# Order of attention blocks, the bank of the last half block and the width of the setup's constant matmuls in a fused attention and feed-forward kernel

## Chip, core and metric

The kernel runs on one core of a Trainium2 chip. The metric is the device time of one execution in microseconds (us), lower is better. Engines are named as in the profile: PE is the matrix engine (TensorE), PEld its weight loads, DVE, ACT and POOL are the vector, scalar and GpSimd engines, SP is the engine that issues most transfers.

## What is computed

Linear attention with decay over 4 batches of 8 heads, 768 positions of 64 elements, followed by a feed-forward layer with a cosine gate over the 3072 resulting rows of 512:

```python
for b in range(nb):                       # blocks of 64 positions
    qb, kb, vb = (q[:, :, sl], k[:, :, sl], v[:, :, sl])
    intra = einsum('bhic,bhjc->bhij', qb, kb) * Dmask        # lam ** (i - j), i >= j
    intra = einsum('bhij,bhjd->bhid', intra, vb)
    inter = einsum('bhid,bhde->bhie', qb * lam_pow, kv_state)
    out[:, :, sl] = intra + inter
    kv_state = lam_block * kv_state + einsum('bhsd,bhse->bhde', kb * rev_pow, vb)
...
h = x @ w_in          # 3072 x 512 by 512 x 2048
g = h * cos(h)
return g @ w_out      # 2048 x 512
```

Inputs and output are float32; matmuls run in bfloat16 with float32 sums.

## The kernel before

The 3072 rows are 24 blocks of 128 rows (6 for each batch), numbered n = 0 to 23. The blocks are grouped into seven tiles, `TILES = [4, 2, 3, 4, 4, 4, 3]`. For each tile i the feed-forward part (`add_ffn`) makes 16 hidden groups (`hidden`, line 577: four matmuls of up to 512 columns into a PSUM bank, then a cosine on ACT at 584 and a product on DVE at 590) and, for each block j of the tile, one output block (`project`, line 620: 16 matmuls in four groups of four, evicted by `project_out`, line 632, and stored by `store_out`, lines 638 and 640). While PE works on tile i, the attention of tile i + 1 is fed in between, block by block.

Attention of a block (`add_attention`): SP loads q, k and v (line 220); POOL scales and casts them (274, 278, 282); q and k are transposed, on PE up to block 7 (300, copied out by DVE at 303), by a transposing DMA from block 8 on (306, into `qkT`); PE multiplies scores (331), DVE masks them (338); PE adds the part from the carried state (356) and the values (360) in bank ps_o, which ACT copies into `xT` (366), the operand of the hidden matmuls; PE updates the state (344), DVE copies it out (350). From block 5 on, the values and update of block n - 1 and the scores of block n are issued as one piece. Buffers for q, k, v and `qkT` are rings of three or four, and the load of block n + 2 is issued after the transposing DMA of block n.

The first four blocks are computed in a setup of their own (`add_span`, lines 432 to 508). It consists of short matmuls with dependencies between engines; while PE would wait in it, it multiplies a constant zero tile (`keep_awake`, line 680, `idle_ps`), so many times as an estimate of the gap holds. The weights are loaded by POOL's queue (250, 253) from 10.36 us on; the loads of block 4 and later follow them on SP, from 32.51 us on.

The order of the work on every engine is written out by a planner. Each piece of work is a `Task` with an engine, an estimated duration, dependencies and a priority; `Planner.order` starts, at each step, the task that can start first by its estimates, and among those that can start at the same time the one with the lowest priority value. Priorities are due times on a common scale: `begins[i]` is the estimated start of tile i, `unit[i]` its estimated length. Hidden group f of tile i is due at `begins[i] + f * unit[i] / 16`, the output blocks of tile i are spread over tile i + 1, and the attention of block n by `prio_attn`, which spreads the blocks of a tile over the tile before it and subtracts 4.0 (line 206). A queue's instructions are issued in the planned order, so a transfer on SP stands behind all that was planned before it.

In the last tile each output block takes another bank (line 605), and the last block of all is cut into two halves of 256 columns (`pieces`, line 607), so that the first half can be evicted and stored while the second is multiplied. Both halves lie in one tile `ps_s` of two banks (line 617), one bank each. DVE evicts the first half, ACT the second.

Of the kernel before, what the change touches and what calls it, by code (L numbers as in the profile page):

```python
# [10 lines left out]
F32 = mybir.dt.float32  # L11
# [5 lines left out]
QK = 4  # L17
THIRD = 1
SPANS = 2
LAG = 2  # L20
ATT = 1.1
TILES = [4, 2, 3, 4, 4, 4, 3]
# [77 lines left out]
def kernel(  # L100
# [10 lines left out]
    nc = tc.nc  # L111
    B, H, S, D = q.shape
    P = 128
# [3 lines left out]
    DM = H * D  # L117
# [4 lines left out]
    first = [sum(TILES[:i]) for i in range(len(TILES) + 1)]  # L122
# [9 lines left out]
    def bank(tag, shape, dt):  # L132
        return psum.tile(shape, dt, tag=tag, bufs=BUFS[tag], name=tag)
# [7 lines left out]
    ident = consts.tile([P, P], BF16)  # L141
    make_identity(nc, ident)
    pos_sp = consts.tile([P, SPANS, 2], F32)
    nc.gpsimd.iota(pos_sp, pattern=[[2 * P, SPANS], [1, 2]], base=-S // 2, channel_multiplier=2,
                   allow_small_or_imprecise_dtypes=True)
# [12 lines left out]
    blank = consts.tile([P, 4 * P], BF16)  # L158
# [3 lines left out]
    for t in kv_bd:  # L162
        nc.vector.memset(t, 0.0)
    lnl = consts.tile([P, H], F32)
    nc.scalar.activation(lnl, lam_bc, AF.Ln)
    expo_sp = consts.tile([P, SPANS, H, 2], F32)
    nc.vector.tensor_mul(expo_sp, pos_sp.unsqueeze(2).to_broadcast([P, SPANS, H, 2]),
                         lnl.unsqueeze(1).unsqueeze(3).to_broadcast([P, SPANS, H, 2]))
    q_sp = consts.tile([P, SPANS, H, 2], F32)
    nc.scalar.activation(q_sp, expo_sp, AF.Exp)  # L170
# [25 lines left out]
    live = {}  # L196


    unit = [MM(n * P, 4 * KF) + MM(DM, KF * n) + ATT * n for n in TILES]
    begins = [sum(unit[:i]) for i in range(len(unit) + 1)]  # L200

    def prio_attn(n, part):
        i = next(i for i in range(len(TILES)) if n < first[i + 1])
        if i == 0:
            return -1000.0 + n + part
        return begins[i - 1] + unit[i - 1] * (n - first[i] + part) / TILES[i] - 4.0

    load_t, issue_t = {}, {}
    last_issue = {}
# [1 line left out]
    def dma(queue, us, issue_us, emit, prio, deps=(), get=None, ordered=True):  # L211
        t = pl.add(queue, issue_us, list(deps) + [last_issue.get(queue) if ordered else None], emit, prio, get=get)
        if ordered:
            last_issue[queue] = t
        d = pl.add("DMA", us, [t], None, prio, lat=1.9)
        d.issue = t
        return t, d
# [47 lines left out]
    def add_attention(n):  # L265
# [43 lines left out]
        if n >= DMA_FROM:  # L309
            first_out, T[n] = dma("SP", 1.2, 1.3, transposes_dma, n - LAG + 1.5, [a, b], get="qkT", ordered=False)  # L310
            T[n].lat = 3.0
            ready = [T[n]]
            if n + LAG < NBLK:
                issue_t["q_f", n + LAG].deps.append(first_out)
        else:
# [244 lines left out]
    def add_ffn(i):  # L560
        nb, n0 = TILES[i], first[i]
        cols = nb * P
        gate = {}


        third = "ps_f" if i == 0 else "ps_t" if i >= THIRD else "ps_h"

        def bank_of(f):
            return third if f % 3 == 1 else "ps_h"

        for f in range(KF):
            pr = begins[i] + f * unit[i] / KF

            def hidden(f=f):
                t = bank(bank_of(f), [P, 4 * P], F32)
                for kd in range(KD):
                    ins = nc.tensor.matmul(t[:, :cols], lhsT=w_in_sb[:, kd, f * P:(f + 1) * P],  # L577
                                           rhs=live["xT", i][:, kd, :cols], start=(kd == 0), stop=(kd == KD - 1))
                live["h", i, f] = t
                return ins  # L580

            def cosine(f=f):
                c = work.tile([P, 4 * P], F32, tag="cos", name="cos")
                nc.scalar.activation(c[:, :cols], live["h", i, f][:, :cols], AF.Sin, bias=halfpi)  # L584
                live["c", i, f] = c

            def gated(f=f):
                if ("g", i) not in live:
                    live["g", i] = work.tile([P, KF, 4 * P], BF16, tag="g", name="g")
                nc.vector.tensor_mul(live["g", i][:, f, :cols], live.pop(("h", i, f))[:, :cols],  # L590
                                     live.pop(("c", i, f))[:, :cols])

            h = pl.add("PE", MM(cols, 4), [Vo[n] for n in range(n0, n0 + nb)] + [w_t["in", f * WCH // KF]],
                       hidden, pr, get=bank_of(f))
            a = pl.add("ACT", 0.26 + cols * 0.000833, [h], cosine, pr, get="cos")
            d = pl.add("DVE", 0.16 + cols * 0.00104, [a] + ([o_last[i - 2]] if i >= 2 else []), gated, pr)
            h.frees = [d]
            a.frees = [d]
            gate[f] = d
            h_last[i] = hid_t[i, f] = h  # L600
        nxt = unit[i + 1] if i + 1 < len(unit) else unit[i]
        U4 = 4
        for j in range(nb):
            last = n0 + j == NBLK - 1
            tag = ("ps_s", "ps_o", "ps_f", "ps_o")[(nb - 1 - j) % 4] if i == len(TILES) - 1 else "ps_f"

            pieces = [slice(0, DM // 2), slice(DM // 2, DM)] if last else [slice(0, DM)]
            evacs, stores = [], []
            store = None
            for piece, part in enumerate(pieces):  # L610
                width = part.stop - part.start
                for f0 in range(0, KF, U4):
                    pr = begins[i + 1] + (j + f0 / KF) * nxt / nb + piece

                    def project(j=j, f0=f0, tag=tag, piece=piece, part=part):
                        if f0 == 0 and piece == 0:
                            live["f", i, j] = ([bank("ps_s", [P, 2, DM], F32)[:, x, :width] for x in range(2)]
                                               if tag == "ps_s" else [bank(tag, [P, DM], F32)])
                        for f in range(f0, f0 + U4):
                            nc.tensor.matmul(live["f", i, j][piece], lhsT=live["g", i][:, f, j * P:(j + 1) * P],  # L620
                                             rhs=w_out_sb[:, f, part], start=(f == 0), stop=(f == KF - 1))

                    t = pl.add("PE", MM(width, U4), [gate[f] for f in range(f0, f0 + U4)] + [w_t["out", f0 * WCH // KF], store],
                               project, pr, get=tag if f0 == 0 and piece == 0 else None)
                    if f0 == 0 and piece == 0:
                        head = t
                    store = t
                o_last[i] = store

                def project_out(eng, j=j, i=i, piece=piece, width=width):  # L630
                    o = live["o_sb", i, j, piece] = work.tile([P, DM], F32, tag="o_sb", bufs=BUFS["o_sb"], name="o_sb")
                    (nc.scalar.copy if eng == "ACT" else nc.vector.tensor_copy)(o[:, :width], live["f", i, j][piece])  # L632

                def store_out(eng, j=j, piece=piece, part=part, width=width):
                    r0 = (n0 + j) * P
                    if n0 + j < 2 * SPANS:
                        for s, h in enumerate(halves):
                            nc.sync.dma_start(out=out[r0 + s:r0 + P:2, :], in_=live["o_sb", i, j, piece][h])
                        return
                    (nc.scalar if eng == "ACT" else nc.sync).dma_start(  # L640
                        out=out[r0:r0 + P, part], in_=live["o_sb", i, j, piece][:, :width])

                eng, queue = ("DVE", "SP") if last and piece == 0 else ("ACT", "ACT" if last else "SP")
                e = pl.add(eng, 0.12 + width / 1060.0, [store], partial(project_out, eng), begins[i + 1] + (j + 1) * nxt / nb,
                           get="o_sb")
                d = dma(queue, 0.7, 0.4, partial(store_out, queue), n0 + j + 8, [e], ordered=False)[1]
                e.frees = [d]
                evacs.append(e)
            head.frees = evacs

    kept = []
    for j, (name, x) in enumerate((("q", 0), ("k", 0), ("q", 1), ("k", 1), ("v", 0), ("v", 1))):
# [5 lines left out]
    for at, name in enumerate(names):  # L658
        which, n = name[0], int(name[1:])
# [16 lines left out]
    idle_ps = bank("ps_h", [P, 4 * P], F32)  # L676

    def keep_awake(us, at):
        for _ in range(int(us / (4 * P / (1200.0 if at < 5.0 else 2400.0) + 0.0025))):
            nc.tensor.matmul(idle_ps, lhsT=ident, rhs=blank, start=True, stop=True)  # L680

    now = 1.6
    for t in pl.order():
# [35 lines left out]
```

## Time and profile before

| what | value |
|---|---|
| median of 11 runs | 219.99 us (219.15 to 222.95) |
| the profiled execution | 219.92 us, its span 218.2 us |
| PE busy | 208.4 us, 95% of the span |
| DVE busy | 122.3 us, 56% |
| ACT busy | 106.6 us, 49% |
| POOL busy | 66.1 us, 30% |
| mean granted PE clock | 0.992 |
| read and written | 27.27 MB and 6.29 MB |
| output matmuls into ps_f, line 620 | 352 of 128x512, 88.7 us |
| hidden matmuls into ps_h, line 577 | 308, 68.3 us |
| constant matmuls, line 680 | 31 of 128x512, 10.8 us |

The span runs from the first to the last instruction; the rest of the execution's time lies around it. Busy time of PE counts overlapping matmuls, so it does not say that each runs at the engine's peak. In the rows of the profile that follow, `x` is a count of instructions, `out<-in` names what is written and read, and a bracket gives the idle time of the engine before the row and what ended it. In rows by slice, each digit is the share of one of 40 equal slices in tenths.

### The profile page before, as it was taken

The page shows a single profiled execution, that of the slowest core. Times are in us where ns is not written, and L with a number is a line of the kernel's source. Part 1 is how long each engine was busy: PE and PEld are TensorE (multiplying, and loading weights), DVE is VectorE, ACT ScalarE, POOL GpSimd, SP SyncE. Part 2 cuts the span into 40 slices and gives each one's busy share as a digit, 9 for nine tenths or more (in the row PEclk, how much of TensorE's full clock was granted, in tenths as well). Part 3 has the DMA queues.
Part 4 walks back from the last instruction along what each step waited for, and adds up shares of the span by engine and source line. Part 5 has one row for each costly group of instructions (what it writes and reads, how often), then busy time and mean ns, then how long its engine had stood idle before and what let it go on. Part 6 is the DMA issues. An engine that isn't in the chain of part 4 may idle for free.

```text
span 218.2 us, 4365 instructions
## 1 busy us (share of the span) xinstructions
PE 208.4 (95%) x1731; PEld 108.7 (50%) x1731; DVE 122.3 (56%) x217; ACT 106.6 (49%) x182; POOL 66.1 (30%) x85
## 2 busy tenths in 40 slices
PE   7896999999999998999999999999999999999993
PEld 2453444455676554454554445455454445555452
DVE  2694578355878877667755564674546334343200
ACT  5682577124474666454545445435444554445320
POOL 4594002786344435454355441300000000000000
PEclk9998899999999999999999999999999999999999
DMA  4999999999899999999899999211001101111112
GB/s 137 347 223 206 204 206 198 238 241 242 205 223 217 222 160 242 218 214 253 165 243 217 232 222 241 51 48 51 20 28 48 51 0 48 48 51 48 48 73 73
DMA packets 93588, 33.84 MB, mean 155 GB/s; under 512 B 80128, under 2 KB 90624, under 8 KB 93568
## 3 DMA queue, kind: packets, MB, share of 16 engines
q1 hardware_dynamic: 89200, 29.24, 57.7%
q0 software_dynamic: 4224, 4.19, 11.8%
q8 instruction: 13, 0.21, 0.4%
q10 hardware_dynamic: 144, 0.13, 0.2%
q14 instruction: 7, 0.06, 0.1%
HBM read 27.27 MB, written 6.29 MB: 154 GB/s over the span
## 4 chain that ended last, share of the span: by engine, by line
PE 80%; DMA 7%; SPq 4%; DVE 3%; ACT 2%; issue 2%; POOL 1%; ACTq 0%
PE ps_f L620 33%; PE ps_h L577 23%; PE ps_t L577 8%; PE ps_s L331 2%; DMA v_f<-in_v_dram 2%; PE ps_f L577 2%; SPq L220 2%; DMA qkT<-qk 2%; PE ps_o L356 2%; SPq L306 2%; PE ps_s L620 2%; PE ps_o L620 2%; DVE s_m_sp L469 2%; PE ps_o L360 2%; DMA q_f<-in_q_dram 1%
## 5 line engine op out<-in xcount | busy, mean ns | idle before, releaser
L620 PE MATMUL ps_f<-w_out_sb,g 128*128 128x512 bf16 x352 | 88.7, 379 | 0.5 <-ACT o_sb L632 0.5
L590 DVE TENSOR_TENSOR g<-ps_h,cos 128x512 bf16<-128x512 f32 (+2 forms) x77 | 47.2, 614 | 46.2 <-ACT cos L584 45.6
L584 ACT ACTIVATE cos<-ps_h,halfpi 128x512 f32<-128x512 f32 (+2 forms) x77 | 48.2, 626 | 48.8 <-PE ps_h L577 46.4
L577 PE MATMUL ps_h<-xT,w_in_sb 128*128 128x512 bf16 (+2 forms) x308 | 68.3, 350 | 0.0
L577 PEld LDWEIGHTS <-w_in_sb 128*128 128x128 bf16 x448 | 43.1, 98 | 41.7 <-issue 1.2
L620 PEld LDWEIGHTS <-g 128*128 128x128 bf16 x400 | 38.0, 98 | 39.8 <-issue 1.5
L274 POOL TENSOR_TENSOR qk<-q_f,q_scale 128x512 bf16<-128x512 f32 x20 | 20.8, 1042 | 54.5 <-DMA q_f<-in_q_dram 33.5
L584 ACT ACTIVATE cos<-ps_t,halfpi 128x512 f32<-128x512 f32 (+2 forms) x30 | 18.5, 616 | 21.3 <-PE ps_t L577 17.9
L338 DVE TENSOR_TENSOR s_m<-ps_s,mask 128x512 bf16<-128x512 f32 x40 | 26.2, 686 | 3.6 <-PE ps_s L331 3.2
L590 DVE TENSOR_TENSOR g<-ps_t,cos 128x512 bf16<-128x512 f32 (+2 forms) x30 | 18.0, 601 | 16.3 <-ACT cos L584 15.7
L577 PE MATMUL ps_t<-xT,w_in_sb 128*128 128x512 bf16 (+2 forms) x120 | 26.5, 344 | 0.0
L282 POOL TENSOR_TENSOR v_s<-v_f,v_scale 128x512 bf16<-128x512 f32 x20 | 20.8, 1042 | 10.5 <-DMA v_f<-in_v_dram 9.5
L632 ACT COPY o_sb<-ps_f 128x512 f32<-128x512 f32 x22 | 12.9, 585 | 19.8 <-PE ps_f L620 19.8
L350 DVE CAST kv_bd<-ps_kv 64x256 bf16<-64x256 f32 x32 | 13.4, 418 | 2.5 <-PE ps_kv L344 1.9
L278 POOL CAST qk<-k_f 128x512 bf16<-128x512 f32 x20 | 12.2, 609 | 2.0 <-DMA k_f<-in_k_dram 2.0
L366 ACT CAST xT<-ps_o 128x512 bf16<-128x512 f32 x20 | 11.6, 581 | 2.4 <-PE ps_o L360 2.3
L680 PE MATMUL ps_h<-blank,ident 128*128 128x512 bf16 x31 | 10.8, 484 | 1.6 <-POOL ident masks.py:199 1.6
L331 PE MATMUL ps_s<-qkT 64*128 64x128 bf16 x160 | 7.9, 219 | 0.8 <-DMA qkT<-qk 0.8
L360 PE MATMUL ps_o<-s_m,v_s 128*64 128x128 bf16 x160 | 7.9, 220 | 0.0
L356 PEld LDWEIGHTS <-kv_bd 128*64 128x64 bf16 x136 | 4.3, 109 | 6.7 <-issue 5.5
L356 PE MATMUL ps_o<-qkT,kv_bd 128*64 128x128 bf16 x136 | 7.0, 225 | 0.0
L360 PEld LDWEIGHTS <-v_s 128*64 128x64 bf16 x160 | 5.5, 110 | 1.3 <-issue 1.3
(88 smaller groups left out, 105.0 us busy)
## 6 DMA issues: line engine op xcount, KB each, us to landing
q_f<-in_q_dram SPq DMA_DIRECT2D x20, 256.0 KB, 3.9
k_f<-in_k_dram SPq DMA_DIRECT2D x20, 256.0 KB, 4.2
v_f<-in_v_dram SPq DMA_DIRECT2D x20, 256.0 KB, 4.6
out_dram<-o_sb SPq DMA_DIRECT2D x19, 256.0 KB, 2.0
w_in_sb<-in_moe_w_in_dram POOLq DMA_DIRECT2D x4, 512.0 KB, 8.7
w_out_sb<-in_moe_w_out_dram POOLq DMA_DIRECT2D x4, 512.0 KB, 14.5
out_dram<-o_sb SPq DMA_DIRECT2D x9, 128.0 KB, 2.5
q_f_sp<-in_q_dram SPq DMA_DIRECT2D x2, 512.0 KB, 5.2
```

The costliest lines, as they stand in the source:

```text
L274: (nc.vector if n == 0 else nc.gpsimd).tensor_mul(live["qk", n][:, 0], live.pop(("q_f", n)), q_scale[:, c, :].unsqueeze(2).to_broadcast([P ...
L282: nc.gpsimd.tensor_mul(live["v_s", n], live.pop(("v_f", n)), v_scale[:, c, :].unsqueeze(2).to_broadcast([P, H, D]))
L331: nc.tensor.matmul(t[:, i, p, :], lhsT=live["qkT", n][h, 1, p, :], rhs=live["qkT", n][h, 0, p, :], start=True, stop=True)
L338: nc.vector.tensor_mul(live["s_m", n][:, i], live["s", n][:, i], mask.unsqueeze(1).to_broadcast([P, NP, P]))
L350: (nc.scalar.copy if early else nc.vector.tensor_copy)(kv_bd[n % NK][h, :, h], kv_ps[h])
L356: nc.tensor.matmul(t[h, p, :], lhsT=kv_bd[(n - 1) % NK][:, p, h], rhs=live["qkT", n][:, 0, p, :], start=(p == 0), stop=False, skip_group_c ...
L360: nc.tensor.matmul(t[h, p, :], lhsT=live["v_s", n][:, 2 * p + i, :], rhs=live["s_m", n][:, i, p, :], start=(p == 0 and c == 0), stop=True, ...
L577: ins = nc.tensor.matmul(t[:, :cols], lhsT=w_in_sb[:, kd, f * P:(f + 1) * P], rhs=live["xT", i][:, kd, :cols], start=(kd == 0), stop=(kd = ...
L584: nc.scalar.activation(c[:, :cols], live["h", i, f][:, :cols], AF.Sin, bias=halfpi)
L590: nc.vector.tensor_mul(live["g", i][:, f, :cols], live.pop(("h", i, f))[:, :cols], live.pop(("c", i, f))[:, :cols])
L620: nc.tensor.matmul(live["f", i, j][piece], lhsT=live["g", i][:, f, j * P:(j + 1) * P], rhs=w_out_sb[:, f, part], start=(f == 0), stop=(f = ...
L632: (nc.scalar.copy if eng == "ACT" else nc.vector.tensor_copy)(o[:, :width], live["f", i, j][piece])
```

## The change

Three edits, in one program.

1. The offset of 4.0 us in the due time of attention becomes a constant `AHEAD`, set to 0.0: the blocks of a tile are spread over the tile before it, from its start to its end.
2. The second half of the last output block takes a bank of its own, in tile `ps_t`, with its own place in the planner's account of banks; the first half keeps the first bank of `ps_s`.
3. The constant matmuls of the setup that are planned to start before 5.0 us have 128 columns instead of 512; their number still fills the same estimated time.

```diff
+AHEAD = 0.0
...
-        return begins[i - 1] + unit[i - 1] * (n - first[i] + part) / TILES[i] - 4.0
+        return begins[i - 1] + unit[i - 1] * (n - first[i] + part) / TILES[i] - AHEAD
...
                         if f0 == 0 and piece == 0:
-                            live["f", i, j] = ([bank("ps_s", [P, 2, DM], F32)[:, x, :width] for x in range(2)]
-                                               if tag == "ps_s" else [bank(tag, [P, DM], F32)])
+                            live["f", i, j] = [bank("ps_s", [P, 2, DM], F32)[:, 0] if tag == "ps_s" else bank(tag, [P, DM], F32)]
+                        elif f0 == 0:
+                            live["f", i, j].append(bank("ps_t", [P, DM], F32))
                         for f in range(f0, f0 + U4):
-                            nc.tensor.matmul(live["f", i, j][piece], lhsT=live["g", i][:, f, j * P:(j + 1) * P],
+                            nc.tensor.matmul(live["f", i, j][piece][:, :width], lhsT=live["g", i][:, f, j * P:(j + 1) * P],
                                              rhs=w_out_sb[:, f, part], start=(f == 0), stop=(f == KF - 1))
...
-                               project, pr, get=tag if f0 == 0 and piece == 0 else None)
-                    if f0 == 0 and piece == 0:
+                               project, pr, get=None if f0 else "ps_t" if piece else tag)
+                    if f0 == 0:
                         head = t
...
-                evacs.append(e)
-            head.frees = evacs
+                head.frees = [e]
...
     def keep_awake(us, at):
-        for _ in range(int(us / (4 * P / (1200.0 if at < 5.0 else 2400.0) + 0.0025))):
-            nc.tensor.matmul(idle_ps, lhsT=ident, rhs=blank, start=True, stop=True)
+        cols = P if at < 5.0 else 4 * P
+        for _ in range(int(us / (cols / (1200.0 if at < 5.0 else 2400.0) + 0.0025))):
+            nc.tensor.matmul(idle_ps[:, :cols], lhsT=ident, rhs=blank[:, :cols], start=True, stop=True)
```

In the program that comes out, the first run of constant matmuls is 41 of 128 columns instead of 10 of 512; the order of PE, DVE, ACT and SP changes from tile 1 on, that of POOL does not.

More of the change, by code (lines that the diff above doesn't have):

```diff
@@ L607, in add_ffn @@
             pieces = [slice(0, DM // 2), slice(DM // 2, DM)] if last else [slice(0, DM)]
-            evacs, stores = [], []
             store = None
@@ L613, in add_ffn, with project @@
                     pr = begins[i + 1] + (j + f0 / KF) * nxt / nb + piece
-                    def project(j=j, f0=f0, tag=tag, piece=piece, part=part):
+                    def project(j=j, f0=f0, tag=tag, piece=piece, part=part, width=width):
                         if f0 == 0 and piece == 0:
-                            live["f", i, j] = ([bank("ps_s", [P, 2, DM], F32)[:, x, :width] for x in range(2)]
-                                               if tag == "ps_s" else [bank(tag, [P, DM], F32)])
+                            live["f", i, j] = [bank("ps_s", [P, 2, DM], F32)[:, 0] if tag == "ps_s" else bank(tag, [P, DM], F32)]
+                        elif f0 == 0:
+                            live["f", i, j].append(bank("ps_t", [P, DM], F32))
                         for f in range(f0, f0 + U4):
-                            nc.tensor.matmul(live["f", i, j][piece], lhsT=live["g", i][:, f, j * P:(j + 1) * P],
+                            nc.tensor.matmul(live["f", i, j][piece][:, :width], lhsT=live["g", i][:, f, j * P:(j + 1) * P],
                                              rhs=w_out_sb[:, f, part], start=(f == 0), stop=(f == KF - 1))
                     t = pl.add("PE", MM(width, U4), [gate[f] for f in range(f0, f0 + U4)] + [w_t["out", f0 * WCH // KF], store],
-                               project, pr, get=tag if f0 == 0 and piece == 0 else None)
-                    if f0 == 0 and piece == 0:
+                               project, pr, get=None if f0 else "ps_t" if piece else tag)
+                    if f0 == 0:
                         head = t
@@ L631, in project_out @@
                     o = live["o_sb", i, j, piece] = work.tile([P, DM], F32, tag="o_sb", bufs=BUFS["o_sb"], name="o_sb")
-                    (nc.scalar.copy if eng == "ACT" else nc.vector.tensor_copy)(o[:, :width], live["f", i, j][piece])
+                    (nc.scalar.copy if eng == "ACT" else nc.vector.tensor_copy)(o[:, :width], live["f", i, j][piece][:, :width])
                 def store_out(eng, j=j, piece=piece, part=part, width=width):
```

## The prediction

> **What bounds the kernel now.** I read the page first (busy shares, clock, DMA), then TensorE's own list of waits, then the timeline of the setup and of the end, and last the transfers around the few places where TensorE waits.
>
> ```profile
> span 218.2 us, 4365 instructions
> ...
> PEclk9998899999999999999999999999999999999999
> DMA  4999999999899999999899999211001101111112
> ...
> q8 instruction: 13, 0.21, 0.4%
> ```
>
> TensorE is busy in every slice, so its stream sets the end, except where the clock row drops (slices 3 and 4) and where it waits. The DMA row is the second resource: full up to slice 24, about 136 us. The last line (packets, MB, share) matters below: 13 packets bring instructions, 0.21 MB / 13 = 16 KB each, for 1731 matmuls and 1731 weight loads, so about 3462 / 13 = 266 instructions, at the most, in a packet.
>
> ```profile
> PE ps_s L494 <- issue: 1.8, 1, 1.8
> ...
> PE ps_s L331 <- DMA qkT<-qk: 0.8, 1, 0.8
> PE ps_s L620 <- DVE o_sb L632: 0.5, 1, 0.5
> ```
>
> Of these waits the first releases on nothing that the profile shows ("issue"), one is on a transposed block that had not landed, one is the last half block. The timeline shows the first:
>
> ```profile
> 16.94 0.90 PE L494 MATMUL ps_s<-s_m_sp,v_sp 64*64 64x128 bf16 x31
> 19.62 0.21 PE L494 MATMUL ps_s<-s_m_sp,v_sp 64*64 64x128 bf16 x1 [1.78 <-issue]
> ...
> 20.40 1.06 PE L680 MATMUL ps_h<-blank,ident 128*128 128x512 bf16 x2
> ...
> 23.95 1.03 PE L577 MATMUL ps_f<-xT,w_in_sb 128*128 128x512 bf16 x4
> ```
>
> TensorE stops in the middle of 32 equal matmuls, one short of the end. The count of instructions by time tells why:
>
> ```profile
> 0.00:10.30 10.30, 7.64 (x64) 3.28 (x65) 4.53 (x13) 6.49 (x12) 5.07 (x15) 1.00 0.80 236
> 0.00:13.19 13.19, 10.53 (x94) 4.77 (x98) 7.42 (x17) 8.98 (x17) 7.89 (x19) 1.00 0.87 245
> 0.00:16.60 16.60, 13.45 (x191) 7.00 (x192) 10.74 (x22) 11.26 (x22) 11.28 (x23) 1.00 0.94 235
> 0.00:19.00 19.00, 14.66 (x223) 7.55 (x224) 12.36 (x25) 11.26 (x22) 13.31 (x25) 1.00 0.98 232
> ...
> 16.57:19.98 3.41, 1.60 (x51) 0.88 (x48) 1.65 (x4) 0.00 (x0) 2.06 (x3) 1.00 1.24 207
> 19.98:23.40 3.42, 3.42 (x35) 1.94 (x30) 1.14 (x3) 1.58 (x4) 0.00 (x0) 0.50 1.25 205
> ```
>
> (Columns: window, length, busy us and count of PE, PEld, DVE, ACT, POOL, clock, DMA share, GB/s.) It stops after 223 + 224 = 447 instructions. The first instruction packet starts at 17.2 us, the second at 23.8 (packet times). [...] The two clock windows show the second loss: after the window with 1.60 us of work in 3.41 the clock is 0.50 for 3.42 us.
>
> **The change part by part.** No computation is added or removed, so I cost only time at TensorE's head.
>
> *Narrower constant matmuls.* 10 of 512 columns become 41 of 128, by the order of the changed program. The ten took 4.45 us at half clock, 0.427 each, so 128 columns take 0.107 and 41 take 4.4: they end near 6.2 instead of 6.06, still before 6.34, when the first transposes begin because VectorE's q_sp arrives (they idled 0.28). If the 41 weight loads were not hidden, up to 41 x 0.107 = 4.4 us more would push the setup; against it, at half clock four 128-column matmuls of L500 with four weight loads took 0.61 with a mean of 0.308 for one, (0.61 - 0.308) / 3 = 0.10 apart. I take 0.
>
> *What the 62 more instructions do.* [...] The second half of L494 must wait for VectorE's s_m_sp until 17.4 anyway, so up to 17.0 costs nothing. Then: L494 done 17.65; VectorE's kv_bd copy ends 17.83, L476 at 17.9; ACT's and VectorE's kv_bd copies (0.36 + 0.43, as now) to 19.2; L500 at 19.25 to 19.65; xT halves on VectorE and ACT (0.42 + 0.37, as now) to 20.53; the third hidden matmul at 20.6, the fourth at 20.8, the next group at 21.02 instead of 23.95: **-2.93 us**. [...]
>
> [...]
>
> *Who is late next.* Tile 0 runs 2.93 earlier, but loads of block 4 onward start at 32.51, behind the weights, and do not move. Block 5: POOL's q copy ends 40.53 and its k copy 42.03; the transposes L300 stand at 43.35 and 44.44 now and would be at 40.43 and 41.69: +0.17 and +0.41. Block 4's k (37.96) hides behind ACT's o_sb copy. Left: 2.93 - 0.58 = **2.35 us**.
>
> *Attention 4 us later.* Summing TensorE's work in the old and new order (0.865 for a group of four 512-column matmuls, 0.65 and 0.44 for 384 and 256), the scores of block 7 move by +2.2, 8 and 9 by +0.9 and +0.4, 10 by +3.7, 11 by +0.9, 12 and 13 by +2.4 and +2.2, **14 by -0.9**, 15 to 17 by +2.6, 18 to 22 by +3.5. The tiles' first hidden matmuls move by at most 0.9. Behind a tile's last values there are 1.65 us of other TensorE work before the next tile (update, scores, one L620 group), more than ACT's xT copy (0.58) behind one cosine (0.69): no new wait.
>
> On SP the stores of output blocks 3, 4 and 5 move ahead of the transposing DMAs of blocks 9, 11 and 14; 256 KB at the 281 GB/s of a full window is 0.9 us, 1.0 taken. Their ACT copies are ready (ends 60.6, 74.7, 86.4 now, less 0.8, 4.3, 1.4 by order, less the lead; SP gets there at 60, 71, 87.5), so no transpose is held up by a waiting store.
>
> ```profile
> 87.00 0.40 PE L331 MATMUL ps_s<-qkT 64*128 64x128 bf16 x8 [0.80 <-DMA qkT<-qk]
> ```
>
> ```profile
> 82.72 2.23 SPq L306 DMA_TRANSPOSE qkT<-qk  x1
> ...
> 87.49 3.07 SPq L306 DMA_TRANSPOSE qkT<-qk  x1
> ```
>
> ```profile
> 79.00:81.00 2.00, 2.00 (x13) 1.08 (x11) 1.94 (x5) 0.58 (x1) 0.00 (x0) 1.00 0.11 8
> 90.00:91.60 1.60, 1.60 (x9) 0.71 (x8) 0.92 (x3) 0.86 (x2) 0.46 (x1) 1.00 1.17 65
> ```
>
> (TensorE's timeline, SP's, and two windows of the transfers.) Transposed blocks 13 and 14 land at 86.95 and 92.82 (landings of the two SP issues at 82.72 and 87.49); block 13's scores are the wait at 87.00. Two pauses of all transfers (8 and 65 GB/s against 220) lie in front of them, 2.5 and 1.7 us by the packets that hang in them. With the lead of 2.35, block 13 is asked for at 86.2 + 2.16 - 2.35 = 86.0: the wait stays, 0.95. Block 14 is asked for at 87.0 + (94.60 - 87.00) - (2.16 + 0.87) = 91.6 and lands at 92.8 to 93.8 (store in front): 1.2 to 2.2 us of new wait. Compared at that point, lead 0.85 to -0.15 is left. Without the pauses both blocks land 2.5 to 4.2 us earlier, neither waits, and 2.35 stays; the 0.8 of before goes too, in both kernels. After block 15 (landed 97.9, asked for near 100) transfers are ahead for good.
>
> *The last half block.*
>
> ```profile
> 212.72 0.42 DVE L632 COPY o_sb<-ps_s 128x256 f32<-128x256 f32 x1 [7.48 <-PE ps_s L620]
> 213.20 1.91 PE L620 MATMUL ps_s<-w_out_sb,g 128*128 128x256 bf16 x16 [0.52 <-DVE o_sb L632]
> ```
>
> Its first matmul now waits for VectorE's copy of the other half, since both lie in one tile, ps_s. 16 matmuls of 256 columns stream in 16 x 0.108 = 1.73: from 210.78 the next can start at 212.51 instead of 213.20, **-0.69**; ps_t was read last near 202. All that follows (ACT copy at 215.19, the last store) moves along; SP's store of the first half (213.2) stays ahead of it.
>
> **Sum.** The profiled execution took 219.92 us (span 218.2, 1.7 around it); the median is 219.99, so I take them as one. With the pauses as traced: 219.92 - 0.69 - (0.85 to -0.15) = 218.4 to 219.4. Without: 219.92 - 0.8 - 0.69 - 2.35 = 216.1. I take the middle, since the runs of before spread over such amounts (219.15 to 221.7 but for one): **217.5 us**, faster by 1.1%. Likeliest case alone: 216.1 to 218.9.
>
> **The rivals.**
> [...]
> B. The setup gains but transfers take it all back at block 14, in most runs: 219.2. For: the DMA row is full to 136 us. Against: pauses must fall into 78 to 92 us.
> C. Slower. The three stores put ahead of transposes delay the stream by 1.0 each and it does not catch up before block 14, which lands at 92.82 + 3.0 = 95.8: lead 26.36 - (95.9 - 67.4) = -2.1 (94.60 less 68.24 us of work before; 67.4 of work now), 219.92 - 0.69 + 2.1 = 221.3. It decides from a landing after 94.7 on. Against: the same bytes pass by then but for one store.
>
> **How the numbers follow.** Forecast 0.66, A 0.11, B 0.14, C 0.09. Half a per cent, 1.1 us, is about what can be told from no change. Faster: 0.66 and 0.04 of A and B, 0.70; same 0.21; slower 0.09. The range 216.0 to 219.5 takes in A, B and the bounds of the pauses and leaves out C.
>
> **What would show it.** No "issue" wait on L494 and a clock of 1.00 from 16 to 24 us; an instruction packet at 14 to 15 us; the first L577 near 20.2 instead of 22.78; L300 of block 5 waiting for POOL; a wait of L331 for qkT near 87 to 94 us, and none of the last L620 for o_sb. Wrong if L494 still stops, if the 41 matmuls run past 6.4 us, or if hidden matmuls wait for xT at the tiles' starts.

## The result, and the profile after

| | before | after |
|---|---|---|
| median | 220.71 us, 50 runs (218.94 to 226.81) | 217.73 us, 13 runs (216.60 to 220.14) |
| ratio after to before | | 0.9884, 95% interval 0.9855 to 0.9912 |
| the profiled execution, its span | 219.92 us, 218.2 us | 220.14 us, 218.4 us |

The change makes the kernel faster by 1.2%. The ratio, here and below, is of the runs within 1.5% of their kernel's fastest, while the medians are of all, and the profiled execution of after is not among the former. It is the slowest of its runs, so it shows more loss than the median holds: the spans before and after are equal within 0.2 us. That makes it useful, for the gain and what ate it are both in it; what it shows of the loss is held beside a second, faster execution further down. The page's head (busy tenths of the clock and of the transfers in 40 slices, then the queue that brings instructions):

```profile
span 218.4 us, 4431 instructions
...
PEclk9999999999999999999999999999999999999999
DMA  4999999998989999999999999131011101111112
...
q8 instruction: 14, 0.23, 0.5%
```

The clock row has lost its dip at slices 3 and 4. The transfers are full as far as before, to their 25th slice. The instruction queue has one packet more. TensorE's waits (what waits, for what: us in all, times, longest):

```profile
PE ps_s L332 <- DMA qkT<-qk: 4.6, 3, 2.0
PE ps_h L681 <- POOL ident masks.py:199: 1.6, 1, 1.6
PE ps_t L444 <- DVE q_sp L433: 0.8, 1, 0.8
```

The stop without a releaser ("issue", 1.8 us) is gone, and so is the wait of the last half block. In their place TensorE waits 4.6 us for transposed blocks, where it waited 0.8. The timeline of TensorE at the setup and at the three waits:

```profile
1.62 3.95 PE L681 MATMUL ps_h<-blank,ident 128*128 128x128 bf16 x41 [1.62 <-POOL ident masks.py:199]
6.42 0.40 PE L444 MATMUL ps_t<-ident,q_sp 128*128 128x128 bf16 x4 [0.85 <-DVE q_sp L433]
...
17.02 0.90 PE L495 MATMUL ps_s<-s_m_sp,v_sp 64*64 64x128 bf16 x32
...
21.23 1.03 PE L578 MATMUL ps_f<-xT,w_in_sb 128*128 128x512 bf16 x4
...
67.38 0.40 PE L332 MATMUL ps_s<-qkT 64*128 64x128 bf16 x8 [1.96 <-DMA qkT<-qk]
...
79.11 0.40 PE L332 MATMUL ps_s<-qkT 64*128 64x128 bf16 x8 [0.96 <-DMA qkT<-qk]
...
89.92 0.40 PE L332 MATMUL ps_s<-qkT 64*128 64x128 bf16 x8 [1.69 <-DMA qkT<-qk]
```

The 32 matmuls of L495 run in one piece, and the second hidden group starts at 21.23 us, 2.72 earlier than the 23.95 of before. The landings of the transposing DMAs (67.34, 79.06 and 89.87 us) name the blocks of the three waits: 9, 11 and 13. The end, on the same timeline:

```profile
211.68 1.91 PE L621 MATMUL ps_s<-w_out_sb,g 128*128 128x256 bf16 x16
...
213.42 1.91 PE L621 MATMUL ps_t<-w_out_sb,g 128*128 128x256 bf16 x16
```

The halves of the last block start 1.74 us apart, where they were 2.42 apart: 0.68 gained. So this execution gained 2.72 + 0.68 = 3.40, paid 4.6 - 0.8 = 3.8 at transposed blocks, and 0.2 went the other way in the rest.

Why block 9 came late stands in SyncE's queue. First before, then after (each row an issue on the queue: start, time until SP goes on):

```profile
56.26 1.35 SPq L306 DMA_TRANSPOSE qkT<-qk  x1
...
58.92 1.03 SPq L220 DMA_DIRECT2D v_f<-in_v_dram  x1
60.12 2.04 SPq L306 DMA_TRANSPOSE qkT<-qk  x1
62.26 1.17 SPq L638 DMA_DIRECT2D out_dram<-o_sb  x2
```

```profile
57.43 1.40 SPq L307 DMA_TRANSPOSE qkT<-qk  x1
...
60.13 2.60 SPq L221 DMA_DIRECT2D v_f<-in_v_dram  x1
62.82 1.50 SPq L639 DMA_DIRECT2D out_dram<-o_sb  x2
64.49 1.33 SPq L307 DMA_TRANSPOSE qkT<-qk  x1
```

Block 9's transpose is issued 4.37 us later. Of these, 1.2 come from the transpose of block 8 in front (57.43 against 56.26), 1.57 from the issue of `v_f` (2.60 against 1.03), and 1.6 from the two stores of output block 3, which stood behind the transpose and now stand before it. Two pauses of the transfers lie in this stretch (87 GB/s from 60.20 to 60.90 us and 67 GB/s from 62.40 to 63.70, where about 200 flow otherwise); that they made the issues slow is likely but not shown.

A second profiled execution of after, of the last group of experiments, took 216.19 us. It has the same two stores ahead of block 9's transpose, but not the rest of the delay: the transpose is issued 1.00 us later than in before, and block 9 waits 0.34 us. The other late block there is 14:

```profile
59.50 1.45 SPq L639 DMA_DIRECT2D out_dram<-o_sb  x2
61.12 2.07 SPq L307 DMA_TRANSPOSE qkT<-qk  x1
```

```profile
65.45 0.40 PE L332 MATMUL ps_s<-qkT 64*128 64x128 bf16 x8 [0.34 <-DMA qkT<-qk]
...
90.69 0.40 PE L332 MATMUL ps_s<-qkT 64*128 64x128 bf16 x8 [0.85 <-DMA qkT<-qk]
```

So the moved stores and waits of 1.2 us in all are common to both executions; the rest of the 4.6 belongs to the slowest one alone.

### The profile page after: what moved, and what is told of

The parts are those of the page before. It is cut to its first block, busy times and chain, and to the rows that moved or that the text cites. A ratio compares the mean times of both kernels' runs of the same rounds, so it can differ in the third digit from the quotient of the medians.

```text
span 218.4 us, 4431 instructions
## 1 busy us (share of the span) xinstructions
PE 206.4 (95%) x1762; PEld 110.4 (51%) x1762; DVE 122.7 (56%) x217; ACT 106.9 (49%) x182; POOL 66.3 (30%) x85
## 4 chain that ended last, share of the span: by engine, by line
PE 61%; DMA 24%; SPq 8%; POOL 5%; issue 1%; ACT 0%; POOLq 0%; ACTq 0%
PE ps_f L621 27%; PE ps_h L578 17%; PE ps_t L578 8%; DMA w_out_sb<-in_moe_w_out_dram 7%; SPq L221 7%; DMA qkT<-qk 6%; DMA v_f<-in_v_dram 5%; DMA q_f<-in_q_dram 4%; DMA k_f_sp<-in_k_dram 3%; PE ps_s L332 2%; PE ps_o L357 2%; PE ps_o L621 2%; PE ps_o L361 1%; POOL w_in_sb L251 1%; POOL v_sp L433 1%
## 5 line engine op out<-in xcount | busy, mean ns | idle before, releaser
L681 PE MATMUL ps_h<-blank,ident 128*128 128x128 bf16 (+1 forms) x62 | 9.6, 318 | 1.6 <-POOL ident masks.py:199 1.6
L332 PEld LDWEIGHTS <-qkT 64*128 64x128 bf16 x160 | 4.5, 94 | 6.3 <-DMA qkT<-qk 5.1
```

What stands on the lines that cost most here:

```text
L332: nc.tensor.matmul(t[:, i, p, :], lhsT=live["qkT", n][h, 1, p, :], rhs=live["qkT", n][h, 0, p, :], start=True, stop=True)
```

## The experiments

They were run in three groups, each beside the kernel before on its own chip, whose medians there were 219.10 (the first four), 219.29 (the next four) and 219.40 us (the last four). "Setup end" is the start of the second hidden group, TensorE's first after the setup, in the profiled run: 23.95 us before, 21.23 after. A ratio is to the kernel before, with its 95% interval.

### Each part alone

**Narrow constants only.** The kernel before with the diff's `keep_awake`.

```diff
-        for _ in range(int(us / (4 * P / (1200.0 if at < 5.0 else 2400.0) + 0.0025))):
-            nc.tensor.matmul(idle_ps, lhsT=ident, rhs=blank, start=True, stop=True)
+        cols = P if at < 5.0 else 4 * P
+        for _ in range(int(us / (cols / (1200.0 if at < 5.0 else 2400.0) + 0.0025))):
+            nc.tensor.matmul(idle_ps[:, :cols], lhsT=ident, rhs=blank[:, :cols], start=True, stop=True)
```

> The kernel before with only the first run of constant matmuls narrowed (41 of 128 columns). Theory (the stop of TensorE in the setup is a block of instructions that comes late, and 62 more instructions ahead of it start its fetch earlier): no issue wait on L494, clock 1.00 from 16 to 24 us, first L577 near 20.4 instead of 22.8. The old order asks for blocks 10, 12 and 13 with no margin, so transfers give back most of the 2.3 us that reach them: 0.2 to 2 us faster, about 1, and more wait of L331 for qkT than the 0.8 of before. Rival (transfers don't matter): 2.5 to 3 us faster. Rival (the stop is tied to something else): it stays, no change.

Measured: 220.70 us (12 runs), ratio 1.0062 (1.0035 to 1.0090): slower, a miss of every theory that paid out the gain of the setup. The stop is gone, as it should be, but the profiled run shows two other things. TensorE's matmuls came up to their full rate late, at 10.88 us (4.78 in after): four constant matmuls of 512 columns from 7.70 us on take 1.91 us, where the same four take 1.03 from 7.55 on in after.

```profile
1.62 4.55 PE L681 MATMUL ps_h<-blank,ident 128*128 128x128 bf16 x41 [1.62 <-POOL ident masks.py:199]
...
18.83 0.90 PE L494 MATMUL ps_s<-s_m_sp,v_sp 64*64 64x128 bf16 x32
...
23.04 1.03 PE L577 MATMUL ps_f<-xT,w_in_sb 128*128 128x512 bf16 x4
```

The 41 matmuls take 4.55 us instead of 3.95, all that follows is later, and the setup ends at 23.04: of the 2.72 us only 0.91 are left, and TensorE gives these back in a wait of 0.99 us for transposed block 10, whose scores start at 70.71 us (70.57 in before, without a wait). And in nine of the twelve runs the mean granted clock is 0.990 to 0.992, in three 1.000 (medians 220.97 and 219.07 us). A half clock over one stretch of 3.41 us lowers the mean over 217 us by 0.5 x 3.41 / 217 = 0.008, so this is one such stretch in a run. Where it lies, the runs without a profile can't show; the half-count and old-order runs below have theirs behind a wait for block 10, so it may well be there. Why this kernel is slower than before, and not merely equal to it, is not shown.

**The last bank only.** The changed kernel with `AHEAD = 4.0` and the old `keep_awake`, so that only the bank of the last half block differs.

> The kernel before with only the bank of its own for the last half block. Theory: the last 16 matmuls start 1.73 us behind the first 16 instead of 2.42, 0.7 us faster at the end, whatever happens ahead of it; by the times of the runs -0.3%, which is hard to tell. Rival (store or eviction of the first half ends last): nothing.

Measured: 218.46 us (12 runs), ratio 0.9957 (0.9925 to 0.9989), 0.6 us. The stop is there (1.4 us, half clock from 19.82 to 23.23), the halves are 1.75 us apart (209.66 and 211.41), and the last half block no longer waits for `o_sb`.

**The order only.** The kernel before without the offset.

```diff
-        return begins[i - 1] + unit[i - 1] * (n - first[i] + part) / TILES[i] - 4.0
+        return begins[i - 1] + unit[i - 1] * (n - first[i] + part) / TILES[i]
```

> The kernel before with only the later attention. Theory: the stop in the setup stays (issue 1.8, clock 0.50 for 3.4 us); the 0.8 us wait for block 13 goes, block 14 is asked for some 1.7 us earlier than before and may wait up to 1; together 0 to 0.8 us faster, within what can be told from no change. Rival (the spreading itself is what makes the change faster): 2 us faster or more.

Measured: 218.54 us (12 runs), ratio 0.9967 (0.9942 to 0.9992). The profiled run has the stop, but not the half clock that the kernel before has after it:

```profile
16.98 0.89 PE L494 MATMUL ps_s<-s_m_sp,v_sp 64*64 64x128 bf16 x31
19.34 0.21 PE L494 MATMUL ps_s<-s_m_sp,v_sp 64*64 64x128 bf16 x1 [1.47 <-issue]
...
22.61 1.03 PE L577 MATMUL ps_f<-xT,w_in_sb 128*128 128x512 bf16 x4
```

The setup ends at 22.61, 1.34 earlier than in before's profile though nothing in the setup was changed; 0.3 of this is the shorter stop (1.47 us against 1.78). So the term of the prediction consists of two: the stop itself, and the half clock that follows in some executions.

### Count or width

**The same count, other widths.** The kernel before with the 62 more instructions, but 8 matmuls of 512 and 33 of 16 columns, so fewer constant columns.

```diff
-        for _ in range(int(us / (4 * P / (1200.0 if at < 5.0 else 2400.0) + 0.0025))):
-            nc.tensor.matmul(idle_ps, lhsT=ident, rhs=blank, start=True, stop=True)
+        n = int(us / (4 * P / (1200.0 if at < 5.0 else 2400.0) + 0.0025))
+        for i in range(41 if at < 5.0 else n):
+            cols = 4 * P if at > 5.0 or i < 8 else 16
+            nc.tensor.matmul(idle_ps[:cols if cols < P else P, :cols], lhsT=ident[:, :cols if cols < P else P], rhs=blank[:, :cols], start=True, stop=True)
```

> The kernel before with a first run of 8 constant matmuls of 512 columns and 33 of 16 columns (with 16-column weights): 41 as in the changed kernel, so 62 more instructions, but 512 columns wide for most of its time, and less constant work in all. Theory (the count of instructions ahead of the stop decides): as e1_narrow_only, no issue wait on L494 and the first L577 near 20.4. Rival (the width of the matmuls, or how busy they keep TensorE, decides): the stop stays, the first L577 near 22.8.

Measured: 219.09 us (12 runs), ratio 0.9993 (0.9965 to 1.0020). No stop, an instruction packet at 12.65 us, the setup ends at 21.17. It is the count of instructions that removes the stop, not what they do. All profiles of this case agree: the five executions with ten wide constants have the stop, the nine with more instructions don't; and where it is, the first instruction packet starts at 16.88 to 17.22 us and TensorE goes on 2.3 to 2.5 us later. The time is nevertheless that of before, and the waits say why:

```profile
PE ps_s L331 <- DMA qkT<-qk: 2.9, 2, 2.7
```

```profile
70.86 0.40 PE L331 MATMUL ps_s<-qkT 64*128 64x128 bf16 x8 [2.68 <-DMA qkT<-qk]
```

This is block 10. Its scores start at 70.57 us in before, without a wait; it had landed just in time, and is late now by what the setup gained. That is what rival B of the prediction says of the time, but in the old order and at block 10 instead of 14. Narrow constants only, with the same count on the same chip, took 1.6 us more (220.70); half-clock stretches are more frequent there (nine of twelve runs under 0.995, here five of twelve), but whether the narrow width brings them is not shown.

**Half the count.** The same, with 5 matmuls of 512 and 20 of 128 columns: 30 instructions more instead of 62.

```diff
...
+        for i in range(25 if at < 5.0 else n):
+            cols = 4 * P if at > 5.0 or i < 5 else P
+            nc.tensor.matmul(idle_ps[:, :cols], lhsT=ident, rhs=blank[:, :cols], start=True, stop=True)
```

> The kernel before with a first run of 5 constant matmuls of 512 columns and 20 of 128: 25, so 30 more instructions, in the same time. [...] A shorter stop than the 2.0 of before either way. Rival (the count does not matter): the stop as before.

Measured: 220.32 us (10 runs), ratio 1.0001 (0.9947 to 1.0055). No stop at all, packet at 12.42 us, setup end 21.25: half the count does all of it, so the packet's start doesn't slide along with the count. The time goes to the same place, and there a second price appears. Windows of this run and of the next one (length, busy us and count of PE, PEld, DVE, ACT, POOL, then clock, DMA share, GB/s):

```profile
67.78:71.19 3.41, 1.41 (x34) 0.99 (x29) 2.45 (x6) 1.06 (x2) 2.29 (x3) 1.00 1.07 230
71.19:74.61 3.42, 3.20 (x11) 1.51 (x10) 1.91 (x4) 1.69 (x3) 2.27 (x3) 0.50 1.15 235
```

TensorE waits 2.00 us for `qkT` of block 10 (to 70.25), and the 3.42 us after that window run at half clock, which costs up to half of them, 1.7 us, more. Here a half clock follows the wait for a transposed block, as it follows the stop in the setup of before (0.50 from 19.98 to 23.40).

### What the order and the stores do

**The changed kernel in the old order.** `AHEAD = 4.0`, all else as after.

> The changed kernel with AHEAD = 4.0, so with narrow matmuls and the bank of its own but the old order. Theory: the lead of the setup runs into transposed blocks 10, 12 and 13, which land with no margin; slower than the changed kernel by 0.3 to 1.5 us, and L331 waits for qkT longer than in the changed kernel. Rival (the order is worth nothing): the same as the changed kernel.

Measured: 219.98 us (10 runs), ratio 1.0011 (0.9976 to 1.0045), mean clock 0.990 to 0.992 in seven of ten.

```profile
68.52:71.93 3.41, 0.87 (x12) 0.57 (x13) 1.55 (x4) 0.26 (x1) 2.01 (x3) 1.00 1.21 249
71.93:75.34 3.41, 3.19 (x11) 1.59 (x11) 1.98 (x4) 1.54 (x3) 1.72 (x3) 0.50 1.30 192
```

The setup ends at 21.21, but TensorE waits 3.1 us for `qkT` (2.87 of them for block 10, to 71.06) and then has its half clock. Two of the three parts, one of them worth 2.7 us in the setup, together gain nothing. With the third they gain 1.2%. In all four kernels that have the setup's gain in the old order, TensorE stands at block 10, and its scores start at 70.25 to 71.06 us, near the 70.57 of before, wherever the setup ended. The later attention is what lets the gain of the setup through: it asks for block 10 later, by 3.7 us in the prediction's count and by 3.3 in the two profiles further down in which no block is late (71.21 and 67.88), and no run of after, of those in the result or in the last group, has a mean clock under 0.997.

**Stores away.** The changed kernel without the stores of output blocks 0 to 5, so rows 0 to 767 of the output are left out.

```diff
+                    if n0 + j < 6:
+                        return
                     r0 = (n0 + j) * P
```

> The changed kernel without the stores of output blocks 0 to 5 (rows 0 to 767 of the output are left out), 1.5 MB less for the transfers to move ahead of block 14. Theory (transfers set when blocks 9 to 14 can be computed): L331 waits for qkT no more or less than 0.5 us in all, 216 to 216.5 us, 1 to 1.5 faster than the changed kernel, and runs spread less. Rival (transposing DMAs are late because of their own chain, POOL's copies and the ring of buffers): the waits stay.

Measured: 216.24 us (4 runs), ratio 0.9866 (0.9781 to 0.9951), no wait for `qkT` in the profiled one. That one (217.31) happened to run its matmuls at the slow rate until 10.95 us (four transposes from 10.61 us in 0.56, from 12.19 in 0.40), with the setup end at 23.37.

**Stores late.** All stores kept, but those of output blocks 0 to 7 are issued behind the last transposing DMA, with 11 buffers `o_sb` so that nothing waits for them. The order of PE, DVE, ACT and POOL is that of after.

```diff
-                d = dma(queue, 0.7, 0.4, partial(store_out, queue), n0 + j + 8, [e], ordered=False)[1]
+                issue, d = dma(queue, 0.7, 0.4, partial(store_out, queue), n0 + j + 8, [e], ordered=False)
+                if n0 + j < LATE:
+                    late_stores.append(issue)
...
+        if t in late_stores:
+            continue
         if t.emit:
             t.ins = t.emit()
+        if t is T[NBLK - 1].issue:
+            for s in late_stores:
+                s.ins = s.emit()
```

> The changed kernel with the stores of output blocks 0 to 7 issued behind the last transposing DMA (11 buffers for o_sb), the order of all other engines unchanged. Theory: as e7_no_early_stores, 216 to 216.5 us, since transfers have room after 137 us; the stores then take some 8 us of SP and are long done by 200. Rival: the late stores collide with the last tiles' stores, or nothing is gained because transfers were not what set the time: 217.7.

Measured: 215.07 us, four runs within 214.91 to 215.14, ratio 0.9812 (0.9751 to 0.9873). The page:

```profile
span 213.2 us, 4387 instructions
...
DMA  4999999999999999999995867188101101111112
```

The transfers are full only to the 21st slice (21 x 5.33 = 112 us), where those of after were to the 25th (136 us), and the stores fill the 27th and 28th, which were nearly idle. Block 9's transpose is issued at 55.58 and lands at 59.62 us, 7.7 earlier than in after, and no wait for `qkT` is left. This kernel beats both: its highest time lies under the lowest of the 17 runs of after, 215.72 us. Its four runs hardly differ, where the thirteen of after spread over more than 3 us (the four of the last group over 1.2). Whether the stores delayed the transposes by their bytes or by their place in SP's queue, these two experiments don't separate: both took away both.

### The parts again, with the transfers out of the way

With late stores the parts can be priced by themselves. These four shared a chip: late stores with the old `keep_awake`, late stores with `AHEAD = 4.0`, after as it is, and the kernel before with late stores and nothing else.

> The changed kernel with the stores of output blocks 0 to 7 issued behind the last transposing DMA (as in the run with 215.07 us), but with the ten constant matmuls of 512 columns again, so 62 instructions fewer ahead of the setup. [...] Rival (the stop is taken up later, the gain is all in the transfers): the stop is there, but the time is 215.0 to 215.7.

> The changed kernel with late stores and with the due times of attention 4.0 us earlier again. Theory (the later attention is worth something only because transposed blocks land late; with the stores out of their way they land in time in the old order too): no wait for qkT over 1 us, no half clock behind the setup, 215.0 to 215.8. Rival (the spread gains by itself, since values and scores fall at better places): 216.5 or more without any wait for qkT. Between: waits for qkT of 1 to 3 us remain, then their sum is the difference.

> The changed kernel as it is, for comparison on the same chip. By the runs so far 217 to 218.5, waits for qkT of 1 to 5 us in all; if its loss against late stores is in these waits alone, time less waits is 214.5 to 215.7.

> The kernel before with only the late stores (old constant matmuls, old order, last half block in the old bank). Theory (the setup's stop and the last bank cost their 2.0 to 2.9 and 0.69 us whatever the transfers do): 217.7 to 218.8, with the stop, with the wait of the last half block, without a wait for qkT. Rival (transfers are the whole story): 215.7 to 216.2.

| kernel | median us (runs) | setup end, us | from there to the last output matmul, us | waits for `qkT`, us |
|---|---|---|---|---|
| all parts, late stores (from above) | 215.07 (4) | 21.21 | 188.91 | none |
| wide constants, late stores | 217.45 (4) | 23.82 | 188.91 | none |
| old order, late stores | 215.93 (4) | 21.15 | 189.72 | none |
| before, late stores | 217.82 (10) | 22.62 | 190.29 | none |
| after | 216.42 (4) | 21.15 | 190.24 | 1.2 |

The first row comes from the other chip; the kernel before took 219.29 there and 219.40 here, which is small beside the differences read from the table. For the old order's the ratios to before say less than the times: 0.9822 (0.9782 to 0.9862) against 0.9812, intervals that overlap.

Wide constants: the stop is back and costs 217.45 - 215.07 = 2.4 us; 2.0 to 2.9 and a time of 217.0 to 218.0 had been expected. Behind the setup nothing differs, 188.91 and 188.91. The timeline of its profiled run:

```profile
16.99 0.89 PE L496 MATMUL ps_s<-s_m_sp,v_sp 64*64 64x128 bf16 x31
19.35 0.21 PE L496 MATMUL ps_s<-s_m_sp,v_sp 64*64 64x128 bf16 x1 [1.47 <-issue]
...
20.79 0.59 PE L502 MATMUL ps_s<-qT_sp,kv_bd 128*128 128x128 bf16 x4
...
22.28 1.70 PE L580 MATMUL ps_h<-xT,w_in_sb 128*128 128x512 bf16 x4
```

The same stop as in the order-only run, 1.47 us, then matmuls at half clock (four of 512 columns in 1.70 instead of 1.02): the setup ends 2.61 later. In before with late stores the stop is the same 1.48, but no half clock follows, and it ends 1.41 later. So the stop alone costs 1.4 us, the half clock 1.2 more.

Old order: 0.9 us more by the medians, across two chips, between the figures of the theory and of the rival, without a wait for `qkT`; by the ratios it is 0.2. The profiles are the better evidence: from the setup's end on both executions in the new order take 188.91 us and this one 189.72, 0.81 longer; before with late stores, less the 0.67 of its last half block (2.42 less 1.75 by the starts), takes 189.62. No wait of TensorE's list accounts for it; where these 0.8 us go stays open. Before: 190.29 less 189.72, 0.57, is left for the last bank; its time lies within what the theory gave. After: 216.42, below what was expected of it. Its profiled run took 216.19, and less its 1.2 us of waits this is 215.0, the time with late stores: in this execution the waits for transposed blocks account for the whole distance.

## Why the prediction was right

It said 217.5 us, and 217.73 was measured. The mechanism is the one it named: a stop in the setup goes, the last half block no longer waits, and late transposed blocks take part of the gain back. That the number came so near is in part luck, since it is the middle of two cases and several terms were off. By its own steps:

- **The stop goes with a late instruction packet, and the count moves both.** Right: shown by the two runs that change the count and not the order. The packet starts at 17.22 us in before and at 12.68 in after, not at 14 to 15. The 14 to 15, and with it that the instructions would be at hand before 17.0, as the -2.93 takes for granted, was the author's estimate; no run shows what a packet's start is to be reckoned from. What the runs show is the packet and, where there is a stop, TensorE going on 2.3 to 2.5 us behind its start. Half of the added instructions moved the packet as far as all of them (12.42 against 12.65 us), so it does not follow the count step by step. It cost nothing here: in after the 32 matmuls of L495 run in one piece from 17.02 us. The kernel with wide constants pays 2.4 us for the stop (2.6 in the profiles, 1.4 for the stop itself and 1.2 for the half clock behind it).
- **-2.93 at the setup's end.** -2.72 in the profile. But that compares with an execution that had the half clock. Of 67 runs of before beside the experiments 35 had a mean clock under 0.995, as one half-clock stretch gives it; without it the stop is worth 1.4. The prediction took one execution for all.
- **41 narrow matmuls at no cost.** They ended at 5.6 us (predicted 6.2), since their rate rose at 4.78, before the end: they start 0.107 us apart up to there and 0.056 apart behind it. (The clock column has 1.00 on both sides; the half clock that the prediction names here is a reading of the matmuls' times, 0.427 us for 512 columns against 0.216 later.) In the two runs where the rate rose near 10.9 the setup ended 1.8 to 2.2 us later. That case was not in the prediction. Both have the narrow constants: two of the seven profiled executions with them rose late and none of the five with wide ones, too few to say whether the width has a part in it.
- **Block 5 waits for POOL, 0.58.** Too large. The transposes L301 stood at 40.85 and 41.94 (predicted 40.6 and 42.1), both 2.50 earlier than in before, so 0.22 of the setup's 2.72 was lost up to there, and no wait for POOL at block 5 is in the list. POOL's copies did not stay where the prediction held them: the k copy ended at 41.34 instead of 42.03, the q copy at 40.78 instead of 40.53.
- **Attention later.** No new wait for `xT` at a tile's start, as said. That the new order is 0.8 us shorter in the profiles without any waits was not foreseen, nor its larger worth: that it lets the setup's gain through.
- **Transfers take back.** The mechanism was right (stores moved ahead of transposes, a transposed block late), its place only in part: in the slowest execution blocks 9, 11 and 13, for 4.6 us in all, in the second one blocks 9 and 14, for 1.2, instead of 13 and 14 for 2.2 to 3.2. Block 9 was late in both: the store moved ahead of it was counted at 1.0 and taken as harmless, and cost 1.6 on the queue. The two executions took 220.14 us, above the case with pauses (218.4 to 219.4), and 216.19, at the case without (216.1). The median fell between them, as the middle of the cases did; that is luck as much as reckoning.
- **The last half block, -0.69.** 0.68 by the starts, 0.57 in the profiles with late stores, 0.64 by the times of the bank alone.
- **Rivals.** A, in which the stop stays, fell: it went. B is what happens to the time in the old order (219.09, 219.98, 220.32 us), at block 10 instead of 14, and not in the new one. C is what happened in the slowest run, at block 9 and with 4.6 us of waits instead of 2.1 of lost lead: 220.14 stands against its 221.3.

## What to carry to other kernels

Here the gain ahead of a full queue lasted only until the next thing that the queue had to deliver: the setup ended 0.9 to 2.8 us earlier in the four kernels of the old order, and the scores of block 10 started at 70.25 to 71.06 us, against 70.57 before. Before counting such a gain, find the first transfer that was just in time, and see what else stands before it in its queue. Parts of a change need not add: alone they gave +0.6%, -0.4% and -0.3%, two together +0.1%, all three -1.2%. Stores that nobody waits for belong behind the loads and transposes that somebody waits for, if buffers allow it; here that was worth another 1.3 to 2.7 us by the medians (215.07 against 216.42 and 217.73, which were not measured beside it; by the ratios 0.9812 against 0.9840 and 0.9884, with intervals that overlap), and its four runs lay within 0.23 us.

## What the runs showed of the hardware

**One wait can be paid twice.** A stop or wait of 1.4 to 2.9 us was followed by 3.41 us at half clock in before, in the bank-only run and in the wide-constants run (stop), and in the half-count and old-order runs (transposed block). It does not always follow: the order-only run and before with late stores had the stop (1.47 and 1.48 us) and no half clock. In after the wait of 1.96 us, from 65.42 to 67.38, gave none:

```profile
62.81:66.22 3.41, 2.61 (x38) 1.74 (x36) 3.04 (x8) 2.23 (x5) 2.16 (x3) 1.00 0.80 199
66.22:69.64 3.42, 2.26 (x19) 1.29 (x20) 1.53 (x3) 0.79 (x2) 0.54 (x2) 1.00 0.90 204
86.70:90.11 3.41, 1.72 (x30) 0.92 (x27) 2.07 (x5) 1.33 (x3) 1.41 (x2) 1.00 1.30 133
90.11:93.53 3.42, 3.42 (x24) 1.52 (x18) 1.91 (x3) 1.17 (x2) 2.26 (x4) 1.00 1.22 291
```

(Windows of after in steps of 3.413 us from 4.78, where its clock record begins. In before's trace the full clock is recorded for 13.653 us, from 6.33 on, and the half clock behind it, from 19.98, for 3.413: the drop lies four such steps behind the start of the record.) In the five profiled runs with a drop the 3.41 us ahead of it held between 0.87 and 1.96 us of TensorE's work (1.60 in before). In after the boundary at 66.22 splits the long wait, and both windows hold over 2.2; the 3.41 us from 65.14, laid across the wait, hold 1.45. Busy time alone doesn't decide: the third window above holds 1.72 us and full clock follows, where 1.96 gave half clock in the bank-only run. What decides stays open.

**Where there is a stop, the first instruction packet starts at 16.88 to 17.22 us, and TensorE goes on 2.3 to 2.5 us later.** In three of the runs without one it starts at 12.42 (half count), 12.65 (same count, other widths) and 12.68 us (after). What starts it is not shown. In before and after the transfers are full from there on (140 to 215 GB/s in each us from 12.3 to 17.3).
